# Moving a skipped general path from the end of a fused attention and two-perceptron kernel to between the two perceptrons

## The chip, the cores and the metric

One core of one Trainium2 chip runs the whole program. Its engines are TensorE (PE: matmuls, with PEld for its weight loads), VectorE (DVE), ScalarE (ACT), GpSimd (POOL) and SyncE (SP, which issues the DMAs here). Every engine has its own instruction stream and runs it in order; engines meet by semaphores. The metric is device microseconds of one execution. The kernel before takes 566.78 us (median of three runs, 566.14 to 567.14).

## The reference

The input is q, k and v of 2 batches, 12 heads, 448 positions and 64 dimensions, a scalar cap (30.0 in the inputs), and the weights of two perceptrons. The weights are float64, the rest float32.

```
scores = q @ k.T / 8
scores = cap * tanh(scores / cap)
attn   = exp(scores - max) ; attn = attn / (sum(attn) + 1e-9)
x = (attn @ v), heads side by side            # 896 tokens x 768
h = x @ w_in1 ; x = (relu(h) ** 2) @ w_out1    # 768 -> 2048 -> 768
h = x @ w_in2 ; x = (h * sigmoid(1.702 h)) @ w_out2
```

## The kernel before, in words

**Attention.** Two heads make one pair; there are 12 pairs. For each pair TensorE computes the scores (`scores`, L359, and the last 64 keys in `tails`, L366) into PSUM banks `bb`, of which there are three double ones; ScalarE applies tanh and, in one instruction of 3136 columns, the exponential (`tanh`, L378 and L380; `exps`, L384). There is no subtraction of the maximum: the bounded path holds for a cap of magnitude up to 64, since then no exponential overflows. TensorE multiplies with v into the one bank `pv` (`weigh`, L391, and `tails`, L369). GpSimd adds the exponentials of a pair over the key chunks (`add`, L400 to L403), TensorE sums the rest with a matmul by ones into the one bank `sm` (`sum_up`, L410; for pair 0 `sum_all`, L419). VectorE takes the reciprocal (`invert`, L429), multiplies (`normalise`, L433) and splits the result into a high and a low part, x_h and x_l (`split`, L90 and L93).

All steps of the attention are put in a list with a time each (`at(t, fn)`), sorted by it, and issued in that order under a manual schedule, so each engine's order is written by hand. A pair is 6.7 units of that time.

**Weights.** The weights arrive as 64-bit words in 64 parts of 128x768. A part runs through the class `Weights`: a DMA on SP (`load`, L123, into two buffers `wraw`), magnitude (L132 on ScalarE, L134 on VectorE), clamp, shift, low word, sign (L140 to L158, all VectorE, tile `wa`, two buffers), then the high part, a rounding copy into `wh` (L86 on ScalarE, L90 on VectorE), and the low part, a subtraction into `wl` on VectorE (L93); `wh` and `wl` have three buffers. The first two parts are finished early in the attention, entirely on VectorE (`merge` and `parts`); the third is begun and finished at the end of it.

**Perceptrons.** Every product is three matmuls, of high and low parts (`mm3`, L102 to L104). `gemm_a` makes, for each of 16 slices of the hidden layer and each batch, one bank of results from x; ScalarE and VectorE apply the activation and split it into g_h and g_l. `gemm_b` runs over the hidden slices in two groups of three output slices; at the end of each group the results are written out: in the first perceptron as new x_h and x_l (`emit_mid`: ScalarE L86, VectorE L93), in the second as output (`emit_out`, stores by SP, L306). Each step takes one finished weight part and prepares another. In one function, `perceptrons`, all four products follow each other; two units of the first perceptron run inside the attention (`ahead`).

**The general path.** For a cap of more than 64 the whole computation is done again by `general_attention` and the perceptrons, with a new `Weights`, inside `tc.If(mag > CAP_BOUND_BITS)` (L608). The cap's bits are loaded into a register of each engine (L606). With the cap of 30 this path is skipped at run time: each engine loads the register, compares and branches over the path's instructions, and executes one semaphore instruction (eight on SP) that waits until the engine's work is done and adds to its semaphores what the skipped instructions would have added. All of this carries line L608 in the profile; what follows behind, the closing meeting of the engines, carries L671. In the program the three stretches lie in this order: the path, the semaphore instructions, what follows. The general path has 3015 instructions of TensorE and 1510 of VectorE.

Of the kernel before, what the change touches and what calls it, by code (L numbers as in the profile page):

```python
# [9 lines left out]
F32R = mybir.dt.float32r  # L10
BF16 = mybir.dt.bfloat16
I32 = mybir.dt.int32
U32 = mybir.dt.uint32
# [6 lines left out]
P = 128  # L20
# [10 lines left out]
WN = 768  # L31
# [10 lines left out]
AHEAD = 2  # L42
# [6 lines left out]
def attn_moe_moe(ctx, tc, qk, v, cap, w1i, w1o, w2i, w2o, out):  # L49
    nc = tc.nc  # L50
# [17 lines left out]
    def all_banks():  # L68
        while True:
            for _ in range(3):  # L70
                t = banks()
                yield t[:, 0, :]
                yield t[:, 1, :]
            yield pv_bank()
            yield sum_bank()

    ring = [all_banks()]
# [17 lines left out]
    def hi_lo(pool, tag):  # L95
        return (
            pool.tile([P, S], F32R, tag=f"{tag}_h", name=f"{tag}_h"),
            pool.tile([P, S], F32R, tag=f"{tag}_l", name=f"{tag}_l"),
        )
# [8 lines left out]
    class Weights:  # L108


        def __init__(self):
            self.todo = [w[j] for w in (w1i, w1o, w2i, w2o) for j in range(16)]
            self.raw = []
            self.cut = []
            self.made = []
            self.whole = []
            self.split = []
            self.ready = []

        def load(self):  # L120
            if self.todo:
                raw = wp.tile([P, WN, 2], U32, tag="wraw", name="wraw")
                nc.sync.dma_start(raw, self.todo.pop(0))  # L123
                self.raw.append(raw)


        def magnitude(self, eng):
            if self.raw:
                raw = self.raw.pop(0)
                a = wp.tile([P, WN], U32, tag="wa", name="wa")  # L130
                if eng is nc.scalar:
                    nc.scalar.activation(a.bitcast(F32), raw[:, :, 1].bitcast(F32), AF.Abs)  # L132
                else:
                    nc.vector.tensor_scalar(a, raw[:, :, 1], 0x7FFFFFFF, None, op0=ALU.bitwise_and)  # L134
                self.cut.append((raw, a))
# [28 lines left out]
        def high_part(self, eng):  # L164
            if self.whole:
                a = self.whole.pop(0)
                h = wp.tile([P, WN], F32R, tag="wh", name="wh", bufs=3)
                l = wp.tile([P, WN], F32R, tag="wl", name="wl", bufs=3)
                rnd(eng, h, a.bitcast(F32))
                self.split.append((h, l, a.bitcast(F32)))  # L170

# [6 lines left out]
    x = {}  # L178
# [33 lines left out]
        act_high(b, fc, gt, pool)  # L212
        act_low(b, fc, gt)

    def perceptrons(w, ahead):
        with ExitStack() as mctx:
            gp = mctx.enter_context(tc.tile_pool(name="gp", bufs=1, reuse_waits="tile"))

            def gemm_a(which, done):
                late = None
                for fc in range(NFC):
                    wt = w.ready.pop(0)
                    pss = {}
                    for b in range(B):
                        if b > 0 or fc >= done:
                            pss[b] = bank()
                            unit_a(pss[b], wt, b)  # L230
                    weights = fc > 0 or not done

                    soon = fc < done
                    if late is not None:
                        gt, ps = act_gate(which, 1, fc - 1, late[:, :S])
                    if weights:
                        w.magnitude(nc.scalar)
                        w.low_word()
                    if late is not None:
                        act_mult(gt, ps)  # L240
                        act_high(1, fc - 1, gt, gp)
                    if weights:
                        w.sign()
                        w.high_part(nc.scalar)
                    if late is not None:
                        act_low(1, fc - 1, gt)
                    if soon:
                        w.low_part()
                    if weights:
                        w.clamp()  # L250
                        w.shift()
                    if 0 in pss:
                        gt, ps = act_gate(which, 0, fc, pss[0][:, :S])
                        act_mult(gt, ps)
                        act_high(0, fc, gt, gp0 if fc < AHEAD else gp)
                    if weights and not soon:
                        w.low_part()
                    if 0 in pss:
                        act_low(0, fc, gt)
                    late = pss[1]  # L260
                activate(which, 1, NFC - 1, late[:, :S], gp)

            def gemm_b(emit):
                for eg in range(2):
                    pss = [[bank(), bank()] for _ in range(3)]
                    for k2 in range(NFC // 2):
                        wh, wl = w.ready.pop(0)
                        for ec in range(3):
                            for b in range(B):
                                for kk in range(2):  # L270
                                    kc = 2 * k2 + kk
                                    j = slice((kk * 3 + ec) * P, (kk * 3 + ec + 1) * P)
                                    mm3(pss[ec][b][:, :S], wh[:, j], wl[:, j], *g[b, kc], kc == 0, kc == NFC - 1)
                        out_ = [(b, ec) for ec in range(3) for b in range(B)] if k2 == NFC // 2 - 1 else []

                        def emit_one():
                            if out_:
                                b, ec = out_.pop(0)
                                emit(b, eg * 3 + ec, pss[ec][b][:, :S])

                        w.magnitude(nc.scalar)
                        w.low_word()
                        emit_one()
                        w.sign()
                        w.high_part(nc.scalar)
                        emit_one()
                        w.clamp()
                        emit_one()
                        w.shift()
                        for _ in range(3):  # L290
                            emit_one()
                        w.low_part()

            def emit_mid(b, ec, ps):
                hh, ll = hi_lo(xp, f"x{b}_{ec}")
                rnd(nc.scalar, hh, ps)
                rest(nc.vector, ll, ps, hh)
                x[b, ec] = hh, ll

            def emit_out(b, ec, ps):  # L300
                o = xp.tile([P, S], F32, tag=f"x{b}_{ec}_h", name="o")
                if b:
                    nc.scalar.activation(o, ps, AF.Copy)
                else:
                    nc.vector.tensor_copy(o, ps)
                nc.sync.dma_start(out[ec * P:(ec + 1) * P, b * S:(b + 1) * S], o)  # L306

            gemm_a(1, ahead)
            gemm_b(emit_mid)
            gemm_a(2, 0)  # L310
            gemm_b(emit_out)

# [3 lines left out]
    def bounded_attention(w, cap_sb, actx):  # L318
# [143 lines left out]
        def at(t, fn, *args):  # L462
            steps.append((t, fn, *args))

        n = NPR
# [33 lines left out]
            w.low_word()  # L499
            w.sign()  # L500

        def parts(eng):
            w.high_part(eng)
            w.low_part()

        def begin():
            w.magnitude(nc.scalar)
# [1 line left out]
            w.shift()  # L509

        at(4.0, merge, nc.vector)
        at(4.1, parts, nc.vector)
        at(9.7, merge, nc.vector)
        at(9.75, parts, nc.vector)
        end = PAIR * (n - 1)
        at(end + 13.0, begin)
        at(end + 18.8, w.low_word)
        at(end + 18.85, w.sign)
# [21 lines left out]
    def general_attention(cap_sb, actx):  # L540
# [9 lines left out]
        for i in range(NPR):  # L550
# [13 lines left out]
            for e in range(2):  # L564
# [25 lines left out]
                    nc.tensor.matmul(pv[:D, :S], vm[:, 2 * kc + e, :], pT[:, kc, :], start=kc == 0, stop=False)  # L590
                nc.tensor.matmul(pv[:D, :S], vl[:, e, :], pT[:TL, KC, :], start=False, stop=True)
                nc.scalar.activation(u[D * e:D * e + D, :], pv[:D, :S], AF.Copy)
            hh, ll = hi_lo(xp, f"x{b}_{n}")
            rnd(nc.gpsimd, hh, u)
            rest(nc.gpsimd, ll, u, hh)
            x[b, n] = hh, ll

    cap_sb = cp.tile([P, 1], F32, name="cap_sb")
    w = Weights()
    with tc.manual_schedule():  # L600
        with ExitStack() as actx:
            bounded_attention(w, cap_sb, actx)
        perceptrons(w, AHEAD)
    bits = cp.tile([P, 1], I32, name="bits")
    nc.vector.tensor_scalar(bits, cap_sb.bitcast(I32), 0x7FFFFFFF, None, op0=ALU.bitwise_and)
    mag = nc.values_load(bits[0:1, 0:1], min_val=0, max_val=0x7FFFFFFF)  # L606

    with tc.If(mag > CAP_BOUND_BITS):  # L608
        ring[0] = all_banks()
        w = Weights()  # L610
        w.load()
        w.load()
        with ExitStack() as actx:
            general_attention(cap_sb, actx)
        for _ in range(2):
            w.magnitude(nc.scalar)
            w.clamp()
            w.shift()
            w.low_word()
            w.sign()  # L620
            w.high_part(nc.scalar)
            w.low_part()
        w.magnitude(nc.scalar)
        w.clamp()
        w.shift()
        perceptrons(w, 0)


# [46 lines left out]
```

## Time and profile before

| | |
|---|---|
| median of 3 runs | 566.78 us |
| profiled execution | 569.99 us |
| its span, first to last instruction | 568.2 us |
| mean granted TensorE clock, share of 2.4 GHz | 0.994 |
| DVE busy | 384.3 us (68%) |
| ACT busy | 259.1 us (46%) |
| POOL busy | 72.3 us (13%) |

The profile is of one execution. A busy share is the time in which an engine executes, and waits on semaphores are left out of it. Matmuls overlap: one is recorded as some 0.36 us long and the next begins 0.2 us later. Register loads, branches and semaphore instructions are not counted as busy; they have records of their own by line, under the engine's name with a q (PEldq is TensorE's sequencer).

### The profile page before, as it was taken

Reading aid. Unit: us, or ns where it says so; the run is one execution under the profiler, and the core shown is the slowest. Engines: PE = TensorE matmul, PEld = TensorE weight load, DVE = VectorE, ACT = ScalarE, POOL = GpSimd, SP = SyncE. Lnnn points to the kernel's source line nnn. Section 1 sums busy time; section 2 is a strip of 40 time slices with the busy share of each in tenths; the row PEclk is TensorE's granted clock in tenths of the full one; section 3 lists DMA queues with packets and bytes.
Section 4 is the critical chain, followed back from the end, with each engine's and each line's share of the span. In section 5 each row is a group of like instructions: output and inputs, shape, how many; then the busy total and the mean of one; then the engine's idle time right before and its main releaser. Section 6 shows DMA issues by size and latency. Waiting matters only on the chain.

```text
span 568.2 us, 6890 instructions
## 1 busy us (share of the span) xinstructions
PE 556.6 (98%) x2755; PEld 464.7 (82%) x2755; DVE 384.3 (68%) x523; ACT 259.1 (46%) x334; POOL 72.3 (13%) x52
## 2 busy tenths in 40 slices
PE   8799999999999999999999999999999999999995
PEld 2233436899999999999999999999999999999995
DVE  3967677899968688553875277777777875376401
ACT  7969993356545453222332255555554432123101
POOL 0669997000000000000000000000000000000000
PEclk9989999999999999999999999999999999999998
DMA  7523210134333333430432123333333253164002
GB/s 256 193 85 110 97 66 2 55 112 166 112 112 112 112 109 118 162 108 27 143 137 97 62 95 112 111 112 111 112 111 112 88 189 113 55 208 165 4 0 103
DMA packets 14727, 61.86 MB, mean 109 GB/s; under 512 B 1760, under 2 KB 4960, under 8 KB 14688
## 3 DMA queue, kind: packets, MB, share of 16 engines
q1 hardware_dynamic: 14544, 61.35, 31.5%
q8 instruction: 23, 0.38, 0.3%
q14 instruction: 16, 0.13, 0.1%
q10 hardware_dynamic: 144, 0.00, 0.0%
HBM read 58.59 MB, written 2.75 MB: 108 GB/s over the span
## 4 chain that ended last, share of the span: by engine, by line
PE 94%; DVE 3%; DMA 1%; ACT 0%; issue 0%; ACTq 0%; SPq 0%; DVEq 0%
PE bb L102 21%; PE bb L103 21%; PE bb L104 21%; PE pv L391 5%; PE pv L103 3%; PE pv L102 3%; PE sm L104 3%; PE sm L102 3%; PE sm L103 3%; PE pv L104 3%; PE bb L359 3%; PE sm L410 2%; PE bb L366 1%; DMA wraw<-w1i 1%; DVE wl L93 1%; DVE wh L90 1%
## 5 line engine op out<-in xcount | busy, mean ns | idle before, releaser
L102 PE MATMUL bb<-x_l,wh 128*128 128x448 f32 x288 | 105.5, 366 | 0.0
L104 PE MATMUL bb<-g_h,wh 128*128 128x448 f32 x288 | 105.2, 365 | 0.0
L104 PE MATMUL bb<-x_h,wh 128*128 128x448 f32 x288 | 105.2, 365 | 0.0
L103 PE MATMUL bb<-x_h,wl 128*128 128x448 f32 x288 | 105.2, 365 | 0.0
L103 PE MATMUL bb<-g_h,wl 128*128 128x448 f32 x288 | 105.2, 365 | 0.0
L102 PE MATMUL bb<-g_l,wh 128*128 128x448 f32 x288 | 105.2, 365 | 0.0
L86 ACT ACTIVATE wh<-wa 128x768 fp32r<-128x768 f32 x62 | 52.5, 846 | 103.5 <-PE bb L104 46.4
L93 DVE TENSOR_TENSOR wl<-wa,wh 128x768 fp32r<-128x768 f32 x64 | 62.7, 980 | 48.2 <-ACT wh L86 48.1
L132 ACT ACTIVATE wa<-wraw 128x768 f32<-128x768 f32 x62 | 56.6, 913 | 65.8 <-DMA wraw<-w2o 18.7
L158 DVE SCALAR_TENSOR_TENSOR wa<-wraw,wa 128x768 uint32<-128x768 uint32 x64 | 60.9, 952 | 1.1
L151 DVE SCALAR_TENSOR_TENSOR wa<-wraw,wa 128x768 uint32<-128x768 uint32 x64 | 60.9, 951 | 0.1
L102 PEld LDWEIGHTS bb<-x_l,wh 128*128 128x128 f32 x288 | 54.1, 188 | 6.4 <-issue 1.4
L86 ACT ACTIVATE g_h<-gt 128x448 fp32r<-128x448 f32 x64 | 37.0, 579 | 45.4 <-DVE gt L199 44.5
L103 PEld LDWEIGHTS bb<-g_h,wl 128*128 128x128 f32 x288 | 54.1, 188 | 4.3
L104 PEld LDWEIGHTS bb<-g_h,wh 128*128 128x128 f32 x288 | 54.1, 188 | 4.3
L102 PEld LDWEIGHTS bb<-g_l,wh 128*128 128x128 f32 x288 | 54.1, 188 | 4.3
L103 PEld LDWEIGHTS bb<-x_h,wl 128*128 128x128 f32 x288 | 54.1, 188 | 4.2
L104 PEld LDWEIGHTS bb<-x_h,wh 128*128 128x128 f32 x288 | 54.1, 188 | 4.2
L199 DVE TENSOR_TENSOR gt<-bb,gt 128x448 f32<-128x448 f32 x48 | 29.7, 619 | 35.4 <-ACT gt L195 23.1
L429 DVE RECIPROCAL r<-sm 128x448 f32<-128x448 f32 x12 | 35.5, 2956 | 18.7 <-PE sm L410 18.7
L140 DVE TENSOR_SCALAR wa<-wa 128x768 f32<-128x768 f32 x64 | 35.4, 553 | 12.0 <-ACT wa L132 12.0
L93 DVE TENSOR_TENSOR g_l<-gt,g_h 128x448 fp32r<-128x448 f32 x64 | 39.5, 618 | 3.1 <-ACT g_h L86 3.1
(84 smaller groups left out, 738.0 us busy)
## 6 DMA issues: line engine op xcount, KB each, us to landing
wraw<-w1i SPq DMA_DIRECT2D x16, 768.0 KB, 4.2
wraw<-w1o SPq DMA_DIRECT2D x16, 768.0 KB, 4.2
wraw<-w2i SPq DMA_DIRECT2D x16, 768.0 KB, 4.1
wraw<-w2o SPq DMA_DIRECT2D x16, 768.0 KB, 4.2
qk<-qk SPq DMA_DIRECT2D x11, 448.0 KB, 3.3
v<-v SPq DMA_DIRECT2D x12, 224.0 KB, 3.5
outT<-o SPq DMA_DIRECT2D x12, 224.0 KB, 2.8
qk<-qk SPq DMA_DIRECT2D x1, 288.0 KB, 3.5
```

Source lines behind the costliest of these rows:

```text
L86: nc.scalar.activation(out_, in_, AF.Copy)
L93: eng.tensor_tensor(out_, in_, hi, op=ALU.subtract)
L102: nc.tensor.matmul(ps, wh, xl, start=first, stop=False)
L103: nc.tensor.matmul(ps, wl, xh, start=False, stop=False)
L104: nc.tensor.matmul(ps, wh, xh, start=False, stop=last)
L132: nc.scalar.activation(a.bitcast(F32), raw[:, :, 1].bitcast(F32), AF.Abs)
L140: nc.vector.tensor_scalar(af, af, LOW, HIGH, op0=ALU.max, op1=ALU.min)
L151: nc.vector.scalar_tensor_tensor(a, raw[:, :, 0], 29, a, op0=ALU.logical_shift_right, op1=ALU.bitwise_or)
L158: nc.vector.scalar_tensor_tensor(a, raw[:, :, 1], 0xC0000000, a, op0=ALU.bitwise_and, op1=ALU.bitwise_or)
L199: nc.vector.tensor_tensor(gt, ps, gt, op=ALU.mult)
L391: nc.tensor.matmul(pvs[i][h, :S], vv[i][:, 2 * c + e, :], t[:, 2 * c + e, :], start=c == 0, stop=i == 0 and c == KC - 1)
L429: nc.vector.reciprocal(r, sums[i][:, :S])
```

## The change

- `tc.If` moves: it stands between the first and the second perceptron. Inside it are the general attention and the first perceptron alone. The second perceptron, common to both paths, follows behind it in a manual schedule of its own. `perceptrons(w, ahead)` becomes `perceptron(w, which, ahead)`.
- The general path uses the bounded path's buffers: `Weights(like=w)` takes w's tiles by name instead of new ones, and `emit_mid` writes the bounded path's x tiles. For this the rings of weight buffers become tiles with a buffer each, named by their number modulo the ring's size.
- The second weight part is no longer finished on VectorE at 9.75 units. Its high part goes to ScalarE at `end + 6.2`, behind the last exponentials, its low part to VectorE at `end + 7.0`.

```diff
-        def __init__(self):
+        def __init__(self, like=None):
+            self.count = {}
+            self.tiles = {}
+            self.like = like
...
+        def tile(self, shape, dtype, name, n):
+            k = self.count[name] = self.count.get(name, -1) + 1
+            tag = f"{name}{k % n}"
+            if self.like:
+                return self.like.tiles[tag]
+            t = self.tiles[tag] = wp.tile(shape, dtype, tag=tag, name=name, bufs=1)
+            return t
...
-                raw = wp.tile([P, WN, 2], U32, tag="wraw", name="wraw")
+                raw = self.tile([P, WN, 2], U32, "wraw", 2)
...
-                h = wp.tile([P, WN], F32R, tag="wh", name="wh", bufs=3)
-                l = wp.tile([P, WN], F32R, tag="wl", name="wl", bufs=3)
+                h = self.tile([P, WN], F32R, "wh", 3)
+                l = self.tile([P, WN], F32R, "wl", 3)
...
-                hh, ll = hi_lo(xp, f"x{b}_{ec}")
+                hh, ll = x[b, ec] = x[b, ec] if w.like else hi_lo(xp, f"x{b}_{ec}")
...
-            gemm_a(1, ahead)
-            gemm_b(emit_mid)
-            gemm_a(2, 0)
-            gemm_b(emit_out)
+            gemm_a(which, ahead)
+            gemm_b(emit_mid if which == 1 else emit_out)
...
         at(4.0, merge, nc.vector)
-        at(4.1, parts, nc.vector)
+        at(4.1, w.high_part, nc.vector)
+        at(4.1, w.low_part)
         at(9.7, merge, nc.vector)
-        at(9.75, parts, nc.vector)
         end = PAIR * (n - 1)
+
+        at(end + 6.2, w.high_part, nc.scalar)
+        at(end + 7.0, w.low_part)
...
-        perceptrons(w, AHEAD)
+        perceptron(w, 1, AHEAD)
...
     with tc.If(mag > CAP_BOUND_BITS):
         ring[0] = all_banks()
-        w = Weights()
-        w.load()
-        w.load()
+        again = Weights(like=w)
+        again.load()
+        again.load()
...
-        perceptrons(w, 0)
+        perceptron(again, 1, 0)
+    ring[0] = all_banks()
+    with tc.manual_schedule():
+        perceptron(w, 2, 0)
```

## Rows read from the trace of the kernel before

**Rows 1.** The page, engines: busy us (share of the span) and instructions.

```profile
PE 556.6 (98%) x2755; PEld 464.7 (82%) x2755; DVE 384.3 (68%) x523; ACT 259.1 (46%) x334; POOL 72.3 (13%) x52
```

**Rows 2.** The chain of waits, 18 to 24 us: start, us, what.

```profile
18.70 2.35 DVE wh L90
...
21.07 2.73 DVE wl L93
```

**Rows 3.** Timeline of PE, 21 to 76 us: start, us, instruction [idle before <-releaser].

```profile
21.48 2.53 PE L359 MATMUL bb<-qk 64*128 64x448 f32 x12
27.46 2.36 PE L391 MATMUL pv<-t,v 128*64 128x448 f32 x8 [3.46 <-DVE sm L433]
...
33.23 2.53 PE L359 MATMUL bb<-qk 64*128 64x448 f32 x12
...
68.70 1.72 PE L391 MATMUL pv<-t,v 128*64 128x448 f32 x8
...
72.87 2.53 PE L359 MATMUL bb<-qk 64*128 64x448 f32 x12
```

**Rows 4.** Stretches: us, busy by engine, PEclk (share of 2.4 GHz), DMA share, GB/s.

```profile
28.40:31.80 3.40, 3.40 (x12) 0.98 (x10) 0.74 (x2) 0.00 (x0) 3.25 (x3) 0.50 0.00 0
...
564.30:568.20 3.90, 0.00 (x0) 0.00 (x0) 0.00 (x0) 0.00 (x0) 0.00 (x0) 0.50 0.06 17
```

**Rows 5.** Timelines of ACT and POOL, 18 to 40 us.

```profile
33.33 0.63 ACT L380 ACTIVATE t<-bb,icap 128x448 f32<-128x448 f32 x1 [6.28 <-PE pv L369]
...
18.36 2.26 POOL L400 TENSOR_TENSOR s<-t 128x896 f32<-128x896 f32 x1 [16.92 <-ACT t L384]
...
25.95 2.07 POOL L400 TENSOR_TENSOR s<-t 128x896 f32<-128x896 f32 x1
...
37.04 2.10 POOL L400 TENSOR_TENSOR s<-t 128x896 f32<-128x896 f32 x1 [4.46 <-issue]
```

**Rows 6.** Timelines of DVE and POOL, 90 to 96 us.

```profile
92.59 2.96 DVE L429 RECIPROCAL r<-sm 128x448 f32<-128x448 f32 x1 [2.90 <-PE sm L410]
...
90.18 2.08 POOL L400 TENSOR_TENSOR s<-t 128x896 f32<-128x896 f32 x1
```

**Rows 7.** Timelines of PE and DVE where the second perceptron begins.

```profile
328.54 0.36 PE L102 MATMUL bb<-x_l,wh 128*128 128x448 f32 x1
...
330.55 0.62 DVE L93 TENSOR_TENSOR x_l<-bb,x_h 128x448 fp32r<-128x448 f32 x1 [0.61 <-ACT x_h L86]
331.10 0.95 DVE L93 TENSOR_TENSOR wl<-wa,wh 128x768 fp32r<-128x768 f32 x1
```

**Rows 8.** Line L606, register loads: ns min/median/max, first and last start us.

```profile
L606 PEldq TENSOR_LOAD <-bits x1: 492/492/492, 558.4 to 558.4; - x1
L606 DVEq TENSOR_LOAD <-bits x1: 818/818/818, 561.0 to 561.0; - x1
```

**Rows 9.** Line L608, branches and semaphore instructions, columns as in rows 8.

```profile
L608 SPq EVENT_SEMAPHORE  x8: 17/17/17, 566.3 to 566.8; - x8
...
L608 PEldq COMPARE_BRANCH  x1: 3682/3682/3682, 559.0 to 559.0; - x1
L608 DVEq COMPARE_BRANCH  x1: 72/72/72, 561.9 to 561.9; - x1
...
L608 SPq COMPARE_BRANCH  x1: 53/53/53, 563.2 to 563.2; - x1
L608 DVEq EVENT_SEMAPHORE  x1: 21/21/21, 565.6 to 565.6; - x1
```

**Rows 10.** Last DVE and PE instructions; stores by line; last store, us to landing.

```profile
561.00 0.62 DVE L305 COPY o<-pv 128x448 f32<-128x448 f32 x1 [0.59 <-PE pv L104]
...
561.81 0.37 PE L104 MATMUL sm<-g_h,wh 128*128 128x448 f32 x1
...
L306 SPq DMA_DIRECT2D outT<-o x12: 332/344/527, 499.6 to 562.8; - x12
...
outT<-o SPq DMA_DIRECT2D x1, 224.0 KB, 2.9
```

More of the change, by code (lines that the diff above doesn't have):

```diff
@@ L129, in magnitude @@
                 raw = self.raw.pop(0)
-                a = wp.tile([P, WN], U32, tag="wa", name="wa")
+                a = self.tile([P, WN], U32, "wa", 2)
                 if eng is nc.scalar:
@@ L213, in activate, with perceptron @@
         act_low(b, fc, gt)
-    def perceptrons(w, ahead):
+    def perceptron(w, which, ahead):
         with ExitStack() as mctx:
@@ L294, in emit_mid @@
             def emit_mid(b, ec, ps):
-                hh, ll = hi_lo(xp, f"x{b}_{ec}")
+                hh, ll = x[b, ec] = x[b, ec] if w.like else hi_lo(xp, f"x{b}_{ec}")
                 rnd(nc.scalar, hh, ps)
                 rest(nc.vector, ll, ps, hh)
-                x[b, ec] = hh, ll
             def emit_out(b, ec, ps):
@@ L500, in merge @@
             w.sign()
-        def parts(eng):
-            w.high_part(eng)
-            w.low_part()
         def begin():
@@ L592, in general_attention @@
                 nc.scalar.activation(u[D * e:D * e + D, :], pv[:D, :S], AF.Copy)
-            hh, ll = hi_lo(xp, f"x{b}_{n}")
+            hh, ll = x[b, n]
             rnd(nc.gpsimd, hh, u)
             rest(nc.gpsimd, ll, u, hh)
-            x[b, n] = hh, ll
     cap_sb = cp.tile([P, 1], F32, name="cap_sb")
@@ L615, in attn_moe_moe @@
         for _ in range(2):
[L616 to L625, printed above, removed]
-        perceptrons(w, 0)
+            again.magnitude(nc.scalar)
+            again.clamp()
+            again.shift()
+            again.low_word()
+            again.sign()
+            again.high_part(nc.scalar)
+            again.low_part()
+        again.magnitude(nc.scalar)
+        again.clamp()
+        again.shift()
+        perceptron(again, 1, 0)
+    ring[0] = all_banks()
+    with tc.manual_schedule():
+        perceptron(w, 2, 0)
 def kernel(**inputs):
```

## The prediction

> **What bounds the kernel now.** I read the engine table first: TensorE is busy 98% of the span [rows 1]. So the time is TensorE's instruction stream plus the places where it stands still, and only those places and the two ends of the run can move. The chain of waits shows the one large hole of the attention: VectorE's two pieces of weight work, 2.35 and 2.73 us, ahead of the reciprocal [rows 2], and TensorE idle for 3.46 us until the normalisation that follows [rows 3]. The clock view adds what the hole costs after it: TensorE ran at 1.2 GHz from 28.4 to 31.8 us, at 2.4 GHz around it [rows 4]. The boundary between the two perceptrons shows no hole at all: the second's first matmul, at 328.54, has no idle time before it [rows 7]. The test of the cap is read last, by its lines: each engine loads the value into a register, branches over the general path, and takes up its next instruction some us later [rows 8, 9]. Today that happens when the work is over.
>
> **Change one: the second part's high and low half go behind the last exponentials.** VectorE loses a cast and a subtraction between 18.70 and 23.80 us. The reciprocal then starts at 18.7 instead of 23.8 and the normalisation ends near 22.4 instead of 27.4, before TensorE has issued its twelve score matmuls (21.48 plus 2.46 of issue, 23.94). TensorE goes on at 23.94 instead of 27.46: 3.52 us. From there to the next scores it takes 33.23 - 27.46 = 5.77 us now, partly at the low clock; later pairs take 72.87 - 68.70 = 4.17, and the earlier ones a little less, 4.1 [rows 3]. That is 1.67 more, 5.2 us together.
>
> What is late next? ScalarE sat idle 6.28 us waiting for TensorE and GpSimd 4.46 us behind it [rows 5]; both move with TensorE. GpSimd's additions then run back to back, as they do from 37.04 us on anyway, at 6.64 us a pair (eight pairs to 90.18 [rows 5, 6]). The first pair took 7.6 us beside VectorE's two pieces, 18.36 to 25.95 [rows 5], and should take 6.65 alone; if it stays slow, GpSimd holds the shift to 4.3. **I take -5.2, with bounds of -4.3 and -5.5.**
>
> The two pieces come back at 87 to 93 us. ScalarE has room for the cast behind its last exponentials. VectorE has 2.90 us of idle time before its reciprocal at 92.59 [rows 6], and the subtraction takes 0.95 us alone [rows 7], but 2.73 beside GpSimd [rows 2]. GpSimd starts an addition at 90.18 that lasts to 92.26 [rows 6], so the subtraction probably ends near 93.1, delays the reciprocal by 0.5, and part of that reaches TensorE. **+0.3, bounds 0 and +0.9.** The Trainium skill ("SBUF — State Buffer") says that VectorE and GpSimd lock a shared port pair and the loser waits for a whole instruction; by that the subtraction waits for the end of one addition, as I took it.
>
> **Change two: the test moves between the perceptrons.** Not run, the general path costs each engine a register load, a far branch and one semaphore instruction, which adds the counts that the skipped code would have added. The general path now writes the same x and weight tiles as the bounded path. So the second perceptron's first matmul, which reads x and a weight, has to wait for the counts of ScalarE and VectorE as they stand after the skipped code, and these appear only when those two engines have passed their own branch. In effect it is a meeting of three engines, where TensorE used to run through.
>
> TensorE's own branch is mostly covered: its sequencer ran 3.4 us ahead of its matmuls (register load at 558.4, last matmul at 561.81 [rows 8, 10]), the branch took 3.68 [rows 9]. VectorE's is not. Its last waiting instruction before the boundary, the last x_l, starts at 330.55; the weight subtraction behind it waits for nothing and starts at 331.10 [rows 7]. At the end of the run the register load began within 0.02 us of VectorE's last instruction (561.00), took 0.82, and the semaphore instruction came at 565.6, 4.6 us after the start [rows 8 to 10]. Counted from 330.57 that is 335.1. The 0.82 ended 0.2 us after the copy beside it; if the load waits for the engine's running work, it ends 0.2 after the subtraction (332.05) and the semaphore comes at 336.0. ScalarE's last instruction is the one for which that x_l waited [rows 7], so ScalarE branches earlier. TensorE restarts 0.1 behind VectorE: 335.2 to 336.1, against 328.54. **A hole of 6.7 to 7.6 us; I take 7.0.** With the shorter fetch of SP (3.1 us from branch to next instruction against 3.7 [rows 9]) and a register load of 0.5 as TensorE's, it would be 5.8.
>
> A hole of 3.46 us was followed by 3.4 us at 1.2 GHz [rows 3, 4], in which work of 1.7 us is done; after the last matmul (ended 562.2) the clock fell at 564.3, inside idle time [rows 4]. Part of a low stretch can lie in the hole, a second can follow it. **+1.3, bounds 0.6 and 2.6.** Behind the restart nothing new is late: the weights of the next step are complete at the boundary, and VectorE and ScalarE start their share with TensorE instead of 3.5 us after it (VectorE is free at 332.05, against the first matmul at 328.54 [rows 7]).
>
> Waiting behind the branches: on ScalarE the next magnitude, on VectorE the low word, on SP the next weight load, which SP issues 5 us after the boundary now. SP's semaphore instructions wait for all its loads, done before 329. GpSimd has nothing. The one-buffer tiles by name replace rings of the same size, with the same readers to wait for: nothing.
>
> **The end.** Now SP issues the last store at 562.8 [rows 10], branches at 563.2, and comes out at 566.3 with eight semaphore instructions, the last at 566.8 [rows 9]. As many closing waits and the meeting of the engines fill the 1.4 us to the span's end at 568.2. The store lands 2.9 us after its issue, at 565.7 [rows 10]. Without the branch SP stands in the closing waits when it lands, past most of them, with about 1.0 of the 1.4 left: 566.7. **-1.6, bounds -1.4 and -2.2** (with the store landing 0.6 us earlier, as no instruction fetch shares the DMA engines then; or all eight closing waits still ahead).
>
> **Sum:** -5.2 + 0.3 + 7.0 + 1.3 - 1.6 = +1.8 us: span 568.2 to 570.0, profiled execution 569.99 to 571.8. The profiled one lies 3.2 above the median of the runs, 566.78; there I expect 568.6.
>
> The Trainium skill ("Advanced Engine Details and Errata", Control Flow Timing) gives a compare-and-branch about 108 ns. By it VectorE would be through at about 331.6, the hole 3.2 us and the sum -3.3, without a low clock. The rows say otherwise: the record of the branch is 0.07 us on VectorE, but the next instruction comes 3.7 us later [rows 9]. "Runtime: NRT & Kernel Launch" (Instruction fetch mechanics) agrees with the rows: a taken branch to a page outside the window waits for its fetch.
>
> **Rivals.**
> *The branch is short or not waited for.* If the first matmuls need no count from behind VectorE's branch, only TensorE's own counts: register load 3.4 us before the last matmul (328.34, one of 0.2 before 328.54), 0.6 to the branch, 3.7 in it [rows 7 to 9]: 329.2, restart at 329.5. Hole 1.0, no low clock: -5.5 us, 561.3. A short branch alone gives -3.3, 563.5. For it: the sequencers run ahead. Against it: both paths write the same tiles. 0.15.
> *The two nearly cancel.* Early bounds at the boundary: hole 5.8, low clock 0.6, end -2.0, subtraction free: -0.8; with a hole of 6.5 about 0: 566 to 567.8. For it: every term sits near its bound in some row. 0.27.
> *The boundary costs more or the attention gives less.* VectorE's load waits for its engine (hole 7.6), the clock stays low for two stretches (2.6), GpSimd holds the shift at 4.3: +4.6 us, 571.4. It decides where the restart after the hole is itself followed by a low stretch. 0.13.
> *Forecast:* slower, 567.9 to 570.2, 0.45.
>
> No change here means within 0.2%, 1.1 us, about what repeated runs can tell. Faster 0.15, same 0.27, slower 0.45 + 0.13 = 0.58. The range runs from 565.6 (inside the first rival) to 570.9.
>
> **What would show it.** Right: no idle time of TensorE before the second pair's pv matmuls and full clock through 24 to 32 us; the first perceptron about 5 us earlier; one hole of 6 to 8 us between the perceptrons that ends right behind VectorE's semaphore instruction of the skipped path, not TensorE's; a low clock around the restart; the span ending about 1 us after the last landing. Wrong: a hole of about 1 us or none, a hole ended by TensorE's own branch, or an attention that is not 4 to 5.5 us shorter.

## The result and the profile after

The changed kernel takes 576.58 us (median of five runs, 571.67 to 580.39), beside 566.78 for the kernel before (five runs, 566.14 to 570.37): ratio 1.0125 [1.0086, 1.0164]. The forecast was 568.6 with a range of 565.6 to 570.9. It had the sign, and missed the size by 8.0 us. A ratio, here and below, leaves out runs that count as slow, so where the times fall into groups (experiments 2, 8 and 12) the list of times says more.

The profiled execution took 575.87 us, span 573.7. The engines' row, against [rows 1], shows TensorE busy for 5.2 us more with the same 2755 matmuls:

```profile
PE 561.8 (98%) x2755; PEld 466.4 (81%) x2755; DVE 382.0 (67%) x522; ACT 260.4 (45%) x335; POOL 72.1 (13%) x52
```

**The attention** went as forecast. PE's timeline (start, us, instruction) has no idle time before the second pair's pv matmuls, where [rows 3] had 3.46 us, and the clock (in the view of stretches, the column before the last two) stays at 1.00 where [rows 4] had 0.50:

```profile
22.29 2.53 PE L371 MATMUL bb<-qk 64*128 64x448 f32 x12
24.75 1.72 PE L403 MATMUL pv<-t,v 128*64 128x448 f32 x8
...
28.82 2.53 PE L371 MATMUL bb<-qk 64*128 64x448 f32 x12
```

```profile
28.00:32.00 4.00, 4.00 (x24) 1.53 (x26) 3.83 (x4) 3.04 (x2) 3.85 (x3) 1.00 0.49 148
```

VectorE's timeline says why: the reciprocal starts at 18.52, where two pieces of weight work stood in [rows 2]. The low part that was moved comes back at 86.21, takes 2.50 beside GpSimd's addition, and the next reciprocal stands right behind it.

```profile
18.52 2.95 DVE L441 RECIPROCAL r<-sm 128x448 f32<-128x448 f32 x1
22.41 0.63 DVE L445 TENSOR_TENSOR sm<-pv,r 128x448 f32<-128x448 f32 x1 [0.94 <-PE pv L403]
...
86.21 2.50 DVE L93 TENSOR_TENSOR wl<-wa,wh 128x768 fp32r<-128x768 f32 x1 [1.00 <-ACT wh L86]
88.64 2.94 DVE L441 RECIPROCAL r<-sm 128x448 f32<-128x448 f32 x1
```

**The first perceptron** began 4.15 us earlier (its stream at 97.84, against 101.99 in the kernel before) and ended no earlier: its last matmul starts at 328.36, before at 328.34 (0.2 ahead of the 328.54 of [rows 7]). PE's timeline of the kernel before at the stream's start:

```profile
101.99 0.47 PE L102 MATMUL bb<-x_l,wh 128*128 128x448 f32 x1
```

The same view of the changed kernel at the stream's start, the two sides of the boundary, and the last matmul of all:

```profile
97.84 0.47 PE L102 MATMUL bb<-x_l,wh 128*128 128x448 f32 x1
...
328.36 0.37 PE L104 MATMUL bb<-g_h,wh 128*128 128x448 f32 x1
334.26 0.71 PE L102 MATMUL bb<-x_l,wh 128*128 128x448 f32 x1 [5.54 <-DVEq L620]
...
569.10 0.37 PE L104 MATMUL bb<-g_h,wh 128*128 128x448 f32 x1
```

Where the lead went is seen when matmuls are counted. The view of stretches gives each engine's busy time and, in brackets, its number of instructions; TensorE is busy throughout and its clock is 1.00 in all four rows. The kernel before, then the changed one, each from 150 to 250 us (first perceptron) and from 400 to 490 (second):

```profile
150.00:250.00 100.00, 100.00 (x495) 92.69 (x494) 75.12 (x112) 44.04 (x67) 0.00 (x0) 1.00 0.35 119
400.00:490.00 90.00, 90.00 (x446) 83.42 (x445) 64.74 (x95) 36.69 (x55) 0.00 (x0) 1.00 0.37 123
```

```profile
150.00:250.00 100.00, 100.00 (x485) 90.83 (x484) 73.13 (x108) 43.00 (x64) 0.00 (x0) 1.00 0.34 116
400.00:490.00 90.00, 90.00 (x446) 83.39 (x445) 66.02 (x97) 38.90 (x58) 0.00 (x0) 1.00 0.35 120
```

485 matmuls instead of 495 in 100 us, with no idle time and no low clock. From start to start a matmul takes 202.7 ns in the kernel before and in the second perceptron, and 206.7 ns in this first one. Four ns times the 1152 matmuls of a perceptron make 4.6 us. I call these the quick and the slow pace. The runs of the changed kernel (these five and six of experiment 4) lie on three steps, two at 571.7 and 572.5, seven at 575.9 to 576.9, two at 580.4 and 581.2. The traces of the runs at 575.87 and 581.19 show one and two slow perceptrons; that both are quick on the lowest step is read from the distance of 4.6 us, since no run of that step was traced.

**The boundary.** The register loads and branches of VectorE, ScalarE and TensorE, by their lines (ns min/median/max, first and last start), answer to [rows 8, 9]:

```profile
L618 DVEq TENSOR_LOAD <-bits x1: 547/547/547, 330.6 to 330.6; - x1
```

```profile
L620 PEldq COMPARE_BRANCH  x1: 5492/5492/5492, 325.5 to 325.5; - x1
...
L620 PEldq EVENT_SEMAPHORE  x1: 51/51/51, 331.0 to 331.0; - x1
L620 DVEq COMPARE_BRANCH  x1: 72/72/72, 331.2 to 331.2; - x1
L620 ACTq EVENT_SEMAPHORE  x1: 17/17/17, 333.0 to 333.0; - x1
L620 DVEq EVENT_SEMAPHORE  x1: 21/21/21, 334.1 to 334.1; - x1
```

TensorE's own branch took 5.49 us, where [rows 9] had 3.68 over the longer body; it comes out of it at 331.0 and stands until VectorE's semaphore instruction at 334.1. The clock is at 1.2 GHz (0.50) for 6.8 us around the restart, half of them inside the hole:

```profile
330.70:334.20 3.50, 0.00 (x0) 0.00 (x0) 1.36 (x2) 0.00 (x0) 0.00 (x0) 0.50 0.05 12
334.20:337.50 3.30, 3.23 (x9) 2.95 (x10) 2.95 (x4) 2.08 (x3) 0.00 (x0) 0.50 0.09 19
337.50:341.00 3.50, 3.50 (x19) 3.25 (x18) 0.00 (x0) 0.97 (x1) 0.00 (x0) 0.99 0.56 209
```

The second perceptron thus starts 5.72 us later than before (334.26 against 328.54) and its last matmul 7.29 later (569.10 against 561.81 of [rows 10]). From there to the span's end it is 4.6 us instead of 6.4.

### The profile page after: what moved, and what is told of

The parts are those of the page before. It is cut to its first block, busy times and chain, and to the rows that moved or that the text cites. A ratio compares the mean times of both kernels' runs of the same rounds, so it can differ in the third digit from the quotient of the medians.

```text
span 573.7 us, 6917 instructions
## 1 busy us (share of the span) xinstructions
PE 561.8 (98%) x2755; PEld 466.4 (81%) x2755; DVE 382.0 (67%) x522; ACT 260.4 (45%) x335; POOL 72.1 (13%) x52
## 5 line engine op out<-in xcount | busy, mean ns | idle before, releaser
L102 PE MATMUL bb<-g_l,wh 128*128 128x448 f32 x320 | 117.3, 367 | 0.0
L104 PE MATMUL bb<-g_h,wh 128*128 128x448 f32 x320 | 117.3, 367 | 0.0
L103 PE MATMUL bb<-g_h,wl 128*128 128x448 f32 x320 | 117.3, 367 | 0.0
L102 PEld LDWEIGHTS bb<-g_l,wh 128*128 128x128 f32 x320 | 60.1, 188 | 5.5
L103 PEld LDWEIGHTS bb<-g_h,wl 128*128 128x128 f32 x320 | 60.1, 188 | 5.5
L104 PEld LDWEIGHTS bb<-g_h,wh 128*128 128x128 f32 x320 | 60.1, 188 | 5.3
```

What stands on the lines that cost most here:

```text
L102: nc.tensor.matmul(ps, wh, xl, start=first, stop=False)
L103: nc.tensor.matmul(ps, wl, xh, start=False, stop=False)
L104: nc.tensor.matmul(ps, wh, xh, start=False, stop=last)
```

## The experiments

**1 to 4: each change alone, and both kernels again on one chip.** On that chip the kernel before had a median of 569.28 (11 runs). Change one alone has only the moved rounding (`tc.If` stays at the end):

```diff
-        at(9.75, parts, nc.vector)
+        at(end + 6.2, w.high_part, nc.scalar)
+        at(end + 7.0, w.low_part)
```

> The kernel before, unchanged, for a second trace of it. In the trace of the changed kernel the matmuls of the first perceptron begin 206.7 ns apart, in its second perceptron and in the whole trace of before 202.7 ns. Theory A (the pace of a stream of matmuls is drawn when the stream starts and stays until the stream stands still): the times of this kernel fall on steps, and the trace shows 202.7 or 206.7 throughout from the first long stream on, 566 us or 570 to 576. Theory B (the slower pace belongs to the changed program: other buffers, other addresses): always 202.7 ns and 566 to 567 us.

Measured: 568.73 median, ratio 0.9994 [0.9955, 1.0032]; runs of 566.2, 566.9, 567.2, 570.3, 570.5 and 578.9. So the kernel before has two levels of its own, some 3.6 us apart. They are not the pace: the profiled run of the upper level (570.54) has 495 and 446 matmuls in the two stretches, the quick pace in both. In the 55 runs beside experiments 5 to 11, 34 lie at 565.8 to 567.4, 19 at 570.0 to 570.7, two between.

> Only the first change: the second weight part's high part behind the last exponentials on ScalarE, its low part behind it; the test of the cap stays at the end. Theory A: the attention is 4 to 5 us shorter (no hole before the second pair's pv matmuls, full clock), so 562 us with the matmuls at 202.7 ns; with both perceptrons at 206.7 ns it would be 9.2 us more (2304 matmuls by 4.0 ns), 571. Theory B: always 562 us. Rival C (the shorter attention is given back by the first perceptron for a reason that lies in the move itself): the first perceptron takes 4 us longer than in the kernel before in every run, 566 us.

Measured: three runs at 565.2 to 565.6 and three at 573.8 to 574.5; ratio of the quick ones 0.9944 [0.9904, 0.9983]. The profiled one (573.83) ran both perceptrons at the slow pace. What follows: the move alone gains, by 4.7 us against the profiled execution of before (569.99) and by 1.4 against the median run, unless the pace is slow.

> Only the second change: the test of the cap between the perceptrons, with the general path on the same buffers; the second weight part finished on VectorE as before. A hole of 5.7 us at the boundary plus 1.7 us for work at the low clock behind it, less 1.8 us at the end: +5.6 us, 572 us with 202.7 ns throughout. Theory A: steps of 4.6 us above that, each perceptron with its own pace, since the stream starts anew behind the hole. Theory B: the first perceptron always at 206.7 ns, the second always at 202.7, 577 us.

Change two with the rounding left where it was. Measured: 572.75, ratio 1.0083 [1.0047, 1.0119], five runs at 571.9 to 573.2 and one at 577.1. Its hole is 5.58 us, its clock low from 330.4 to 333.8. The test between the perceptrons costs about 6 us against the runs near 566.8.

> The changed kernel, unchanged, for a second trace. Theory A: times on steps of about 4.6 us (571.5, 576, 580.5), by which of the two perceptrons runs at 206.7 ns; the trace need not show the same perceptron slow. Theory B: the first perceptron at 206.7 ns and the second at 202.7 in this trace too, 576 us.

The changed kernel itself. Measured: 576.71, ratio 1.0126 [1.0089, 1.0163]; its profiled run (581.19) has 486 matmuls in the first stretch and 437 in the second, against 495 and 446 before: both perceptrons slow.

```profile
150.00:250.00 100.00, 100.00 (x486) 90.87 (x485) 73.28 (x108) 42.46 (x64) 0.00 (x0) 1.00 0.34 115
400.00:490.00 90.00, 90.00 (x437) 81.78 (x437) 66.83 (x100) 38.52 (x58) 0.00 (x0) 1.00 0.34 115
```

The first perceptron did not begin slow in this run. Its first 72 matmuls are 202.7 ns apart; then TensorE waits some 0.15 us for the low part of the fourth weight part, and from 112.96 on they are 206.7 apart. PE's timeline at that wait:

```profile
112.29 0.36 PE L102 MATMUL pv<-x_l,wh 128*128 128x448 f32 x1
112.65 0.47 PE L103 MATMUL pv<-x_h,wl 128*128 128x448 f32 x1
```

**5: whose turn comes first at 18.6 us.** One small GpSimd addition more in the kernel before, ahead of the first pair's sum:

```diff
+            if i == 1:
+                nc.gpsimd.tensor_tensor(s[:, 0, :192], t[:, 0, :192], t[:, 2, :192], op=ALU.add)
```

> The kernel before, with one more GpSimd addition of 192 columns ahead of the first pair's sum, so that VectorE's cast at 18.6 us gets its turn ahead of the 6.28 us of additions. Theory (which of the two comes first decides the two levels of the kernel before, about 566.7 and 570.3 us): the cast takes about 0.6 us and the subtraction 2.8 us, TensorE waits 0.9 us instead of 3.5 at 27.5 us, its clock is not low from 28.4 to 31.8 us, and all runs lie at 566.5 to 567.5 us, but for one in ten some 4.6 us above from the slow pace of the matmuls. Rival (the two levels of before come from something else, as the pace): times at both levels again, and a median of 568 to 570 us even where the wait is short.

Measured: 567.12, ratio 0.9977 [0.9953, 1.0002]; eleven runs at 566.7 to 567.4, none at 570 (the twelfth, 613.65, had a clock of 0.851 over its whole span). The cast comes first and takes 0.84 us, and TensorE waits 2.06 us instead of 3.77 in experiment 1; I had expected 0.6 and 0.9. Timelines of VectorE in experiment 1 and of VectorE and TensorE in this one:

```profile
19.11 2.33 DVE L90 CAST wh<-wa 128x768 fp32r<-128x768 f32 x1
21.47 2.73 DVE L93 TENSOR_TENSOR wl<-wa,wh 128x768 fp32r<-128x768 f32 x1
```

```profile
18.70 0.84 DVE L90 CAST wh<-wa 128x768 fp32r<-128x768 f32 x1
19.57 2.73 DVE L93 TENSOR_TENSOR wl<-wa,wh 128x768 fp32r<-128x768 f32 x1
```

```profile
25.97 1.72 PE L391 MATMUL pv<-t,v 128*64 128x448 f32 x8 [2.06 <-DVE sm L435]
```

The kernel before without the added instruction shows the same in experiment 11, whose attention is unchanged and whose profiled run lay on its lower level (567.45). There the cast starts ahead of the addition by itself and takes the 0.56 us of an undisturbed one, and the hole is 1.09 us, about as I had expected. The clock is 1.00 from 24 to 36 us. Timelines of VectorE and TensorE in experiment 11:

```profile
18.57 0.56 DVE L90 CAST wh<-wa 128x768 fp32r<-128x768 f32 x1
```

```profile
25.57 1.72 PE L394 MATMUL pv<-t,v 128*64 128x448 f32 x8 [1.09 <-DVE sm L436]
```

So the upper level of the kernel before is the execution in which the addition takes its turn ahead of the cast, with the long hole and the low clock behind it. The execution that I forecast from was one of these; the median of 566.78 belongs to the others.

**6: the same branch with little to jump over.** The If's body becomes a copy of each x_h and x_l onto itself:

```diff
-        ring[0] = all_banks()
-        again = Weights(like=w)
...
+        for hh, ll in x.values():
+            nc.scalar.activation(hh, hh, AF.Copy)
+            nc.vector.tensor_copy(ll, ll)
```

> The changed kernel with the body of the If cut down to one copy of each x_h onto itself on ScalarE and of each x_l on VectorE; it leaves out the general path for caps above 64, which this input does not take. Theory (the hole of 5.7 us behind the first perceptron is in the main the jump over the body's many instructions: VectorE's next event came 2.9 us behind its branch, TensorE's branch record lasted 5.5 us): the hole shrinks to 2.5 to 3.5 us, and the time, at equal pace of the matmuls, is 2 to 3 us under the changed kernel's: 569 where both perceptrons run fast, 573.6 with one slow, 578 with both. Rival (the cost is the engines' meeting and the load of the register, whatever the body's length): the hole stays at 5.3 to 5.8 us and the times at 571.7, 576.5 and 580.5 us.

Measured: 574.54, ratio 1.0126 [1.008, 1.0172], on steps again: 570.7 and 571.0, three at 574.0 to 575.2, one at 578.7. On the quick step that is 1.3 us under the changed kernel (570.8 against 572.1). The hole is 3.99 us, between the two expectations, with 1.1 us from VectorE's branch to its semaphore instruction instead of 2.9:

```profile
L620 PEldq COMPARE_BRANCH  x1: 228/228/228, 321.0 to 321.0; - x1
L620 ACTq COMPARE_BRANCH  x1: 45/45/45, 326.3 to 326.3; - x1
L620 ACTq EVENT_SEMAPHORE  x1: 17/17/17, 326.4 to 326.4; - x1
L620 DVEq COMPARE_BRANCH  x1: 72/72/72, 326.9 to 326.9; - x1
...
L620 DVEq EVENT_SEMAPHORE  x1: 21/21/21, 328.0 to 328.0; - x1
```

Timelines of VectorE and TensorE:

```profile
327.01 0.95 DVE L93 TENSOR_TENSOR wl<-wa,wh 128x768 fp32r<-128x768 f32 x1
```

```profile
328.17 0.71 PE L102 MATMUL bb<-x_l,wh 128*128 128x448 f32 x1 [3.99 <-DVEq L620]
```

What follows: the far jump adds 1.5 us to a hole of 5.5. The other 4.0 are the meeting: the last outputs' way through ScalarE and VectorE, the register load, and a weight subtraction on VectorE that ended 0.04 us ahead of its semaphore instruction. That subtraction hides a part of the jump. ScalarE, which had no work left, went from its branch to its semaphore instruction in 0.1 us over the short body and in 2.5 us over the long one.

**7: many new starts for the stream.** Change one alone, with a matmul of 64 columns ahead of each unit of batch 1 in the first halves (16 a perceptron; the expectation counted twice as many):

```diff
+                            if b == 1:
+                                nc.tensor.matmul(pss[b][:, :64], wt[0][:, :P], x[b, 0][1][:, :64], start=True, stop=True)
                             unit_a(pss[b], wt, b)
```

> Change one alone (If at the end, the second part's rounding moved), with one more matmul of 64 columns ahead of the 18 of each unit of batch 1 in the perceptrons' first halves: 32 a perceptron, whose result is overwritten. Theory (the pace of 202.7 or 206.7 ns a matmul is drawn when the even stream of 448-column matmuls begins, and kept until something breaks it): stretches of both paces in one trace, each beginning behind one of the small matmuls; the runs lie within 3 us of each other instead of in two groups 9 us apart, at 565.3 + about 3 us for the 64 small matmuls + up to 9.2 us by the share of slow stretches. Rival (the pace is set once a run, by the place of the instructions or by the clock): one pace in the whole trace, and two groups of times near 568 and 577 us.

Measured: 569.15, ratio 1.0019 [0.9996, 1.0042], all twelve runs within 568.5 to 569.9. Each small matmul costs 0.11 us, 3.5 in all on top of 565.3. The mixture that I expected is not there. The stream begins at 97.7 with the first small matmul, right behind the attention's matmuls and without idle time; its first 18 matmuls of 448 columns ran at 206.4 ns, and every stretch behind a later small matmul at 202.5 to 202.7. Behind a small matmul inside a running stream no draw is seen: in the one trace all such stretches are quick.

**8 and 11: does the wait at 117 us make the kernel before quick?** In it TensorE waits 0.15 us for a low part there, and its stream starts again. Both kernels compute that low part twice, number 8 on change one alone, number 11 on the kernel before:

```diff
                     if soon:
+                        if which == 1 and fc == 1:
+                            h, l, f = w.split[0]
+                            rest(nc.vector, l, f, h)
                         w.low_part()
```

> Change one alone, with the low part of the fourth weight part computed twice on VectorE, 0.96 us longer, so that TensorE stands still for about 1.1 us at 112 us and its stream begins again there, as it did in the kernel before at 117 us. Theory (the pace is drawn at such a start, and a start behind a wait for the low part draws the quick pace in most runs, 20 of 22 of the kernel before): at least four of six runs near 566.3 us, the others near 575.5. Rival (a start behind a wait draws either pace alike, and the kernel before owes its quick runs to something else): about half of the runs near 575.5 us, as with change one alone.

Measured: three runs at 566.3 to 567.1, nine at 574.9 to 576.4 (ratio 1.0036 [0.998, 1.0091], which describes neither group). The theory falls: a start behind a wait draws the slow pace too, as the trace of experiment 4 shows directly.

> The kernel before with the low part of the fourth weight part computed twice, so that TensorE's wait at 117 us lasts about 1.1 instead of 0.15 us; nothing of the change. Theory (which pace is drawn hangs on when the wait ends against TensorE's own steps, so the kernel before has its quick pace from the length of its wait): a good part of the runs 9 us above the others, as with change one and the same hold, 9 of 12. Rival (the slow pace comes with the order of change one, whatever the wait): all but one run in ten at 567.2 to 568.0 or 570.8 to 571.5 us, the two levels of the kernel before plus 1.

Measured: 567.6, ratio 1.0017 [0.9994, 1.004], nine runs at 567.4 to 568.0 and three at 570.6 to 571.5; none of twelve slow. The rival holds: the slow pace comes with the order of change one, not with the length of this wait. That it comes with this order alone is not shown, since one run of experiment 3 (577.1) and two of the kernel before (578.9 and 581.7, none of the three traced) lie as high.

**9 and 10: the pace forced to quick.** The small matmul of experiment 7, at three places of the changed kernel (the diff shows these), and at the first two of them in change one alone:

```diff
+                            if b == 1 and (which, fc) in ((1, 1), (1, 3), (2, 1)):
+                                nc.tensor.matmul(pss[b][:, :64], wt[0][:, :P], x[b, 0][1][:, :64], start=True, stop=True)
```

> The whole change, with three more matmuls of 64 columns (results overwritten), each ahead of a unit of batch 1 inside a running stream: the second and the fourth unit of the first perceptron and the second of the second. Theory (the time beyond the forecast is the slow pace of 206.7 ns that a stream keeps until it is broken, and a small matmul inside the stream sets it back to 202.7): each costs 0.11 us, every run lies at 571.8 to 573.0 us, none at 576.5 or 580.5, and both perceptrons show 202.7 ns behind the small matmuls. Rival (the excess of the slower runs is something else that comes with the change, as memory traffic or the instruction supply): the groups near 572, 576.5 and 580.5 us stay.

Measured: 571.82, ratio 1.0068 [1.0043, 1.0093], nine runs at 570.9 to 573.5; the steps at 576.5 and 580.5 are gone, and with them the rival. In the second perceptron the break can be watched. PE's timeline: 40 steps from 334.23 to 342.49 make 206.5 ns each, 40 from 343.20 to 351.31 make 202.8:

```profile
334.23 0.37 PE L103 MATMUL bb<-x_h,wl 128*128 128x448 f32 x1
...
342.49 0.37 PE L104 MATMUL bb<-x_h,wh 128*128 128x448 f32 x1
342.70 0.19 PE L246 MATMUL bb<-x_l,wh 128*128 128x64 f32 x1
...
343.20 0.36 PE L104 MATMUL bb<-x_h,wh 128*128 128x448 f32 x1
...
351.31 0.36 PE L102 MATMUL bb<-x_l,wh 128*128 128x448 f32 x1
```

> Change one alone with two of these small matmuls, in the second and the fourth unit of the first perceptron: the version that the runs so far point to. Theory: every run at 565.3 + 0.22 + 0.1 = 565.4 to 566.2 us, none near 574.5, so under the kernel before's median of 567 to 569 and a little under its quicker level of 566.3. Rival as above: half of the runs near 574.5 us.

Measured: 566.1, ratio 0.9966 [0.9945, 0.9988], eleven runs at 565.4 to 566.8 (the twelfth took 1427 us at full clock and stays unexplained). Its first stream began slow (16 steps from 98.51 to 101.81, 206 ns each) and was quick behind the small matmul. This version, without the test moved, is quicker than both kernels, by 0.3% against the kernel before.

**12: ScalarE or the place.** Change one alone, with the second part rounded on VectorE at the new time:

```diff
-        at(end + 6.2, w.high_part, nc.scalar)
+        at(end + 6.2, w.high_part, nc.vector)
```

> Change one alone, but the second part's high word is still rounded on VectorE, at the new time, and not on ScalarE. Theory (the slow pace comes with the place of the move, behind the last exponentials, whichever engine rounds): the runs fall in two groups as with change one alone, some at 565.2 to 566.5 us and a third or more at 574 to 576. Rival (it comes with ScalarE's added rounding ahead of the last pair's work): no run over 568 us.

Measured: 568.05, ratio 1.0019 [0.9982, 1.0057]; ten runs at 567.8 to 568.7, two at 576.2. Neither expectation fits: by the times the slow pace occurs without ScalarE's rounding, but less often, and the kernel is 2.6 us slower on the quick step than with it. The times do not show every slow start. The profiled run is one of the ten (567.93), and still its stream began slow: 70 steps from 99.82 to 114.28 make 206.6 ns each, 40 from 114.90 to 123.00 make 202.7. It turned quick in the middle, with no idle time of TensorE and no small matmul. The one irregular step there is a weight load that started 0.07 us late, behind the low part that it reads. Timelines of VectorE and of TensorE's weight loads:

```profile
113.56 0.96 DVE L93 TENSOR_TENSOR wl<-wa,wh 128x768 fp32r<-128x768 f32 x1 [0.38 <-ACT wh L86]
```

```profile
114.29 0.19 PEld L102 LDWEIGHTS pv<-x_l,wh 128*128 128x128 f32 x1
114.57 0.19 PEld L103 LDWEIGHTS pv<-x_h,wl 128*128 128x128 f32 x1
```

In the changed kernel's profiled run the same load was 0.08 us late (112.90 instead of 112.82), and the pace stayed slow. So such a delay can end the slow pace and need not.

## Why the prediction was wrong

**The sum came out; its last line did not.** The sum was +1.8 us on the profiled execution, 571.8. On its lowest step the changed kernel takes 571.7 to 572.5, and 571.5 by experiment 9 (571.82 less three small matmuls). Luck has a part in that: the hole was forecast 1.3 us too long and the attention's gain 0.75 us too large, and these two errors offset each other in part. The step that failed stands at the sum's end: "The profiled one lies 3.2 above the median of the runs, 566.78; there I expect 568.6." These 3.2 us were no constant offset. They are the very hole that change one removes, which the median run of the kernel before does not have at that length (experiments 5 and 11). I took its gain of 5.2 us off an execution that had it, and then took the difference off again. Against the median run change one is worth 1.4 us (experiment 2), not 4.9. That is 3.2 of the 8.0 us.

**No term had the pace.** The other 4.8 us are one perceptron at 206.7 ns a matmul, in the median run. I had taken TensorE's stream as fixed and looked only at the places where it stands still; that is the second step that failed, a term put at nothing. The one trace that I had ran at the quick pace throughout and gave no reason to ask. Experiments 7, 9 and 10 show it by its removal. Why the streams behind change one start slow so often is open. By the traces, the first perceptron's stream began slow in six of nine with change one and in none of five without it. By the times, a slow pace lasted in three of six runs of experiment 2, nine of twelve of 8, two of twelve of 12, and at most in the two of 89 runs of the kernel before that lie above 572 us. It is not the length of the wait at 117 us (experiment 11).

The other terms, from the profiled execution:

- *Attention*, -5.2 and +0.3 for the moved pieces: -4.15 at the first perceptron's stream, and -4.9 in experiment 2 (97.13 against 101.99). The mechanism was as written. The Trainium skill ("SBUF — State Buffer", SBUF: two separate sides) says that a GpSimd instruction and a VectorE instruction of some kinds hold a shared port pair for a whole instruction, whoever starts first. The traces agree: the same cast takes 0.56 us (experiment 11) when it starts ahead of the addition and 2.33 (experiment 1) when it starts behind it. What I did not draw from it is that such an order can change from run to run.
- *Hole*, +7.0 (6.7 to 7.6, 5.8 at the low end): 5.7 as I had counted it, from start to start (5.5 idle), just under the low end, with the engine that I had named ending it. The register load took 0.55 us, not 0.82, and VectorE's semaphore instruction came 2.9 us behind its branch, not 3.7. TensorE's own branch took 5.49 us, not 3.68, and still ended 3.1 us ahead of VectorE's semaphore instruction. The far jump adds only 1.5 us to the hole (experiment 6). The first rival, that nothing waits for VectorE's branch, is out.
- *Low clock*, +1.3: 1.6, the later last matmul (7.29) less the later start (5.72).
- *End*, -1.6: -1.8.

The Trainium skill ("Advanced Engine Details and Errata", Control Flow Timing) has 108 ns for a compare-and-branch. The records here are shorter, 72 ns on VectorE and 45 to 50 on ScalarE, but the next instruction comes later: on ScalarE 0.1 us over the short body and 2.5 over the long one, on VectorE 2.9 over the long one.

## What to carry to other kernels

Before a gain from one profiled execution is set against the median of the runs, ask whether that execution is of the median's kind: a wait that hangs on which of two engines takes its turn first is there in some runs and not in others, and the difference between levels may be the gain itself. A stream of even matmuls is a term of its own: count matmuls over a long stretch of busy time before and after, since a 2% change of pace shows neither as idle time nor as clock. A test in the middle cost more here by the meeting that it forces on the engines (4.0 us) than by what the far jump adds (1.5 us).

## What was not expected of the hardware

An even stream of 448-column matmuls, each with its own weight load, has two paces at full clock, 202.7 and 206.7 ns. It takes one when it starts, behind a standstill (the boundary), a short wait (experiment 4) or the attention's matmuls, and kept it for up to 2268 matmuls (experiment 2). It can also change in a stream without idle time, as in experiment 12, so the pace is not always kept to the stream's end. One matmul of 64 columns inside the stream, for 0.11 us, set it back to the quick pace at all four places where a trace shows it slow before (experiments 7, 9 and 10). At the very start of the stream, directly behind the attention's matmuls, it did not (97.7 us in experiment 7). What decides the pace at a start is open.
